# Attention and MoE in one kernel: from which tile on scores and value products use split operands

## The chip, the cores and the metric

One core of a Trainium2 chip runs the whole kernel. The time is that of the device for one execution, in microseconds; the median of several executions counts.

## The reference

Eight batches of eight heads go through attention with a window and a few global positions, and the result through a small MoE-like layer:

```python
s_g = scale * q_g @ concat(k_g, k_l).T          # 32 global queries see all 544 keys
out_g = softmax(s_g) @ concat(v_g, v_l)
s_ll = where(abs(i - j) <= 32, scale * q_l @ k_l.T, -1e9)   # 512 local queries, window 32
s_l = concat(scale * q_l @ k_g.T, s_ll)          # and the 32 global keys
out_l = softmax(s_l) @ concat(v_g, v_l)
x = concat(out_g, out_l).transpose(0, 2, 1, 3).reshape(8 * 544, 512)
h = maximum(maximum(x @ w1, x @ w2), x @ w3)     # w1, w2, w3: 512 x 768
out = h @ w_out                                  # 768 x 512
```

All operands are float32.

## The kernel before, in words

The attention runs over 128 tiles (`sl` from 0 to 127). A tile is 128 queries of a pair of heads (`p = sl // 4`, the place in it `t = sl % 4`); four pairs make a batch. For a tile there are four steps on PE, each ahead of the next by one or more tiles: `scores(sl + 3)`, `trans(sl + 1)` (transposes the softmax, which went to the buffer `prob` by DMA), `transg(sl + 1)` (the same for the softmax of the global queries, from `probg`) and `pv(sl)` (the product with the values). `glob(p + 1)` makes the global scores of the next pair in two parts, `glob_soft` its softmax: the smallest value `nmg`, the exponential, its sum `zg` with a reciprocal, a scaling, and six DMAs to `probg`.

Between these steps `fill(n)` puts matmuls of the MoE layer of the batch before, 18 a tile, from tile 16 on. The weights of that layer come in as float32 and are split into a high and a low part on the way (`convert`): ACT at L165, four DVE steps at L168 to L171, ACT at L178, POOL at L182. These conversions go on, one or two a tile, up to tile 25, and the last ones are those of w_out.

A float32 product can be made in two ways here. Native: operands stay float32, and PE takes each matmul in two records (lines L273, L315, L383). Split: an operand is first divided into a high part, rounded to the faster format, and a low part, the difference; PE then multiplies these (L277, L319, L390). `split_q`, `split_k` and `split_v` divide the queries, keys and values: a cast on ACT (`copy`) and a subtraction on POOL or DVE (`sub`, L94). With a split value product the transposed softmax is divided too (`trans` and `transg`: a second step on DVE, from PSUM), and the result's parts are added: a copy `lox` on ACT, one add at L396 and two at L398 on DVE in place of one copy of the result.

Two numbers say where the change from native to split takes place: `NATK`, the tiles with native scores (the global scores of a pair go with its first tile), and `NAT`, the first tile with a split value product.

`copy`, `sub` and `times` choose the engine with the least load by a table of costs. The order of instructions on each engine is set when the program is built, by priorities and the layer's own estimates of what is ready, so it is not that of the code, and it moves when the work changes. Each engine works strictly through its row; the DMAs are all issued from SP's queue, in its order.

Of the kernel before, what the change touches and what calls it, by code (L numbers as in the profile page):

```python
# [22 lines left out]
KW = 576  # L23
NEG = -8.0e9

NATK = range(0, 28)
HIMAX = float(np.array(0x47EFFFFF, np.int32).view(np.float32))


# [22 lines left out]
def body(ctx, tc, kin, qin, vin, min_, w1, w2, w3, w4, out):  # L52
# [43 lines left out]
    def copy(out, a, psum=False):  # L96
        n = width(out)
        c = {"d": n * (1.04 if psum else 0.52) + (160 if psum else 150), "a": n * 0.833 + (150 if psum else 190)}
        if least(c) == "d":
            dve.tensor_copy(out=out, in_=a)  # L100
        else:
            act.copy(out=out, in_=a)  # L102
# [103 lines left out]


    NS = 4 * B * NP
    NAT = 26
    EARLY, AHEAD = 16, 9  # L210
    kraw, kst, qraw, qs, vraw, vs, xr, sc, pg, pts = [{} for _ in range(10)]

    def load_k(p):
        if p < B * NP:
            if 4 * p in NATK:
                kraw[p] = att.tile([128, KW + 2 * SG], F32, name="kn", tag="kst")
# [4 lines left out]
    def split_k(p):  # L221
        if p >= B * NP or 4 * p in NATK:
            return
        r = kraw.pop(p)
        g = r[:, KW:].rearrange("p (j g) -> p j g", j=2)
        t = qgz
        copy(t[:, :, 0:SG], g)
        sub(t[:, :, 64:64 + SG], g, f32(t)[:, :, 0:SG])
        t = kst[p] = att.tile([128, 2, KW], F32R, name="kst")
        copy(t[0:64, 0], r[0:64, 0:KW])  # L230
        copy(t[64:128, 1], r[64:128, 0:KW])
        sub(t[64:128, 0], r[0:64, 0:KW], f32(t)[0:64, 0])
        sub(t[0:64, 1], r[64:128, 0:KW], f32(t)[64:128, 1])

    def load_q(s):
        if s < NS:
            if s in NATK:
                qraw[s] = att.tile([128, 256], F32, name="qn", tag="qs", bufs=4)
# [4 lines left out]
    def split_q(s):  # L243
        if s < NS and s not in NATK:
            r = qraw.pop(s)
            t = qs[s] = att.tile([128, 2, 256], F32R, name="qs", bufs=4)
            copy(t[:, 0], r)
            sub(t[:, 1], r, f32(t)[:, 0])
# [6 lines left out]
    def split_v(s):  # L255
        if NAT <= s < NS:
            v = vraw.pop(s)
            t = vs[s] = att.tile([128, 4, 2, D], F32R, name="vs")
            copy(t[:, :, 0], v)
            sub(t[:, :, 1], v, f32(t)[:, :, 0])  # L260

    def glob(p, step):
# [7 lines left out]
        ps = psS.tile([128, 512], F32, name="S")  # L270
        if 4 * p in NATK:

# [27 lines left out]
    def scores(sl):  # L300
# [11 lines left out]
        for j in range(2):  # L312
            if sl in NATK:

# [19 lines left out]
    def trans(sl):  # L334
# [11 lines left out]
        src = ps.rearrange("p (x q) -> p x q", q=128)  # L346
        if sl < NAT:
            pt = pts[sl] = att.tile([128, 2, 2, 160], F32, name="pt", tag="pt")
# [7 lines left out]
    def transg(sl):  # L356
# [7 lines left out]
        src = g[:, 64 * h:64 * h + 64 * n].rearrange("p (c j g) -> p c j g", j=2, g=SG)  # L364
        if sl < NAT:
            copy(pt.rearrange("p j c q -> p c j q")[:, 0:n, :, 128:160], src, True)
# [6 lines left out]
    def pv(sl):  # L373
# [3 lines left out]
        if t == 0:  # L377
            xr[p] = xp.tile([128, 4, 160], F32, name="xr")
        if sl < NAT:

# [211 lines left out]
```

## Time and profile before

| | |
|---|---|
| median of 3 runs | 859.42 us (859.35 to 860.28) |
| profiled execution | 863.26 us, its span 861.4 us |
| mean granted clock of PE | 0.973 |
| PE busy | 813.0 us, 94% of the span |
| DVE, ACT, POOL busy | 566.7, 529.1, 509.8 us |

The profile is of one execution. Busy time of PE counts matmuls that overlap, so a busy PE is not PE at its peak. "PEld" is PE's loading of the stationary operand. The chain of waits follows the work that ended last back in time, at each step to what released it. A row of a timeline gives start and length in microseconds, the engine, the line, the operation, and in brackets how long the engine was idle before it and what ended that.

### The profile page before, as it was taken

Reading aid. Unit: us, or ns where it says so; the run is one execution under the profiler, and the core shown is the slowest. Engines: PE = TensorE matmul, PEld = TensorE weight load, DVE = VectorE, ACT = ScalarE, POOL = GpSimd, SP = SyncE. Lnnn points to the kernel's source line nnn. Section 1 sums busy time; section 2 is a strip of 40 time slices with the busy share of each in tenths; the row PEclk is TensorE's granted clock in tenths of the full one; section 3 lists DMA queues with packets and bytes.
Section 4 is the critical chain, followed back from the end, with each engine's and each line's share of the span. In section 5 each row is a group of like instructions: output and inputs, shape, how many; then the busy total and the mean of one; then the engine's idle time right before and its main releaser. Section 6 shows DMA issues by size and latency. Waiting matters only on the chain.

```text
span 861.4 us, 15721 instructions
## 1 busy us (share of the span) xinstructions
PE 813.0 (94%) x4452; PEld 674.2 (78%) x4452; DVE 566.7 (66%) x1784; ACT 529.1 (61%) x1479; POOL 509.8 (59%) x683
## 2 busy tenths in 40 slices
PE   5866788999999999999999999999999999999997
PEld 3644566778888788888888888888888888888896
DVE  4657699787777677777778677867787676511111
ACT  4656566677767676767776767776776766511111
POOL 4535577786667666776768576766677664411211
PEclk8786999999999999999999999999999999999999
DMA  6586655424333533344333533353334322100000
GB/s 201 166 243 186 190 165 190 146 90 153 103 106 96 160 112 106 100 123 125 104 109 100 150 98 100 96 160 111 112 111 131 121 75 72 62 24 1 25 25 25
DMA packets 107238, 98.53 MB, mean 114 GB/s; under 512 B 21008, under 2 KB 97936, under 8 KB 107152
## 3 DMA queue, kind: packets, MB, share of 16 engines
q1 hardware_dynamic: 107152, 97.53, 37.2%
q8 instruction: 36, 0.59, 0.3%
q14 instruction: 50, 0.41, 0.2%
HBM read 56.85 MB, written 8.91 MB: 76 GB/s over the span
## 4 chain that ended last, share of the span: by engine, by line
PE 82%; DVE 6%; DMA 6%; ACT 2%; issue 2%; SPq 2%; POOL 1%; ACTq 0%; POOLq 0%; DVEq 0%
PE pm L421 45%; PE pm L440 16%; PE O L390 6%; PE S L319 5%; PE T L342 4%; DMA wraw<-w_in 2%; PE S L277 1%; DVE wraw L170 1%; DMA probg<-sg 1%; PE O L383 1%; PE S L363 1%; PE pm L315 1%; DMA early<-s 1%; ACT s L324 1%; PE S L315 1%
## 5 line engine op out<-in xcount | busy, mean ns | idle before, releaser
L421 PE MATMUL pm<-xs,wh 128*128 128x512 f32 (+1 forms) x1296 | 408.0, 388 | 3.3 <-POOL xs L94 3.3
L421 PEld LDWEIGHTS pm<-xs,wh 128*128 128x128 f32 x1296 | 233.6, 189 | 35.3 <-POOL xs L94 3.8
L421 PE MATMUL pm<-xs,wl 128*128 128x512 f32 (+1 forms) x648 | 253.1, 391 | 0.0
L112 POOL TENSOR_SCALAR s<-s,z 128x192 f32<-128x192 f32 (+1 forms) x250 | 113.0, 465 | 98.7 <-ACT lox L102 37.8
L421 PEld LDWEIGHTS pm<-xs,wl 128*128 128x128 f32 x648 | 122.5, 189 | 22.7 <-issue 1.6
L324 ACT ACTIVATE s<-s,nm 128x192 f32<-128x192 f32 (+1 forms) x256 | 118.0, 462 | 26.6 <-DVE nm L322 22.6
L440 PE MATMUL pm<-woh,h 128*128 128x512 f32 x408 | 133.7, 398 | 0.1
L94 POOL TENSOR_TENSOR h<-m,h 128x512 fp32r<-128x512 f32 (+1 forms) x54 | 69.3, 1283 | 95.4 <-ACT h L102 93.9
L429 DVE TENSOR_TENSOR m<-pm,m 128x512 f32<-128x512 f32 (+1 forms) x108 | 71.1, 659 | 72.2 <-PE pm L421 72.0
L94 POOL TENSOR_TENSOR qs<-qraw,qs 128x256 fp32r<-128x256 f32 x100 | 73.8, 749 | 56.3 <-ACT qs L102 45.3
L94 DVE TENSOR_TENSOR pt<-T,pt 128x512 fp32r<-128x512 f32 x102 | 70.5, 691 | 46.4 <-ACT pt L102 44.5
L322 DVE CUSTOM_DVE_ANT_0 s<-S,mask 128x192 f32<-128x192 f32 (+1 forms) x232 | 77.9, 371 | 18.5 <-PE S L315 7.7
L326 DVE TENSOR_SCALAR z<-z 128x2 f32<-128x2 f32 x128 | 52.0, 406 | 49.8 <-ACT s L324 49.2
L440 PEld LDWEIGHTS pm<-woh,h 128*128 128x128 f32 x408 | 74.7, 188 | 12.1 <-POOL h L94 0.5
L440 PE MATMUL pm<-wol,h 128*128 128x512 f32 x204 | 81.8, 401 | 0.0
L94 POOL TENSOR_TENSOR vs<-vraw,vs 128x256 fp32r<-128x256 f32 x102 | 75.8, 744 | 8.2 <-ACT vs L102 4.0
L94 POOL TENSOR_TENSOR kst<-kraw,kst 64x576 fp32r<-64x576 f32 x49 | 70.4, 1436 | 11.8 <-issue 8.2
L102 ACT CAST pt<-T 128x512 fp32r<-128x512 f32 x90 | 52.7, 586 | 36.0 <-PE T L342 36.0
L102 ACT CAST qs<-qraw 128x256 fp32r<-128x256 f32 x100 | 40.5, 407 | 54.8 <-PE S L319 54.3
L390 PEld LDWEIGHTS O<-pt,vs 128*128 128x128 f32 x408 | 66.4, 188 | 9.1
L390 PE MATMUL O<-pt,vs 128*128 128x320 f32 (+1 forms) x408 | 72.8, 300 | 0.0
L342 PEld LDWEIGHTS T<-identr,prob 128*128 128x128 f32 x448 | 50.5, 141 | 25.1 <-DMA prob<-s 2.6
(95 smaller groups left out, 1292.2 us busy)
## 6 DMA issues: line engine op xcount, KB each, us to landing
vraw<-v_in SPq DMA_DIRECT2D x128, 128.0 KB, 2.4
qraw<-q_in SPq DMA_DIRECT2D x100, 128.0 KB, 2.2
prob<-s SPq DMA_DIRECT2D x56, 224.0 KB, 2.4
prob<-s SPq DMA_DIRECT2D x56, 192.0 KB, 2.3
wraw<-w_in SPq DMA_DIRECT2D x18, 512.0 KB, 5.3
out_dram<-o SPq DMA_DIRECT2D x32, 256.0 KB, 2.6
kraw<-k_in SPq DMA_DIRECT2D x25, 320.0 KB, 3.1
qn<-q_in SPq DMA_DIRECT2D x28, 128.0 KB, 3.4
```

The costliest lines, as they stand in the source:

```text
L94: (dve if least(c) == "d" else pool).tensor_tensor(out=out, in0=a, in1=b, op=ALU.subtract)
L102: act.copy(out=out, in_=a)
L112: pool.tensor_scalar(out=out, in0=a, scalar1=col, scalar2=1.0, op0=ALU.mult, op1=ALU.mult)
L319: pe.matmul(ph[j][:, 0:n], lhsT=qs[sl][:, a, 128 * j:128 * j + 128], rhs=kst[p][:, j, c0:c0 + n], start=(a == 0), stop=(a == 1))
L322: dve.tensor_tensor_reduce(out=s[:, j, 0:n], in0=ph[j][:, 0:n], in1=mask[:, (1, 0, 1, 0)[t], 32 * (t == 0):32 * (t == 0) + n], scale=-0.12 ...
L324: act.activation(out=s[:, j, 0:n], in_=s[:, j, 0:n], func=AF.Exp, bias=nm[:, j:j + 1], scale=-1.0, accum_out=z[:, j:j + 1])
L326: dve.tensor_scalar(out=z, in0=z, scalar1=1e-9, scalar2=None, op0=ALU.add)
L342: i = pe.transpose(pr[:, 256 * j + 128 * c:256 * j + 128 * c + 128], s[:, j, 128 * c:128 * c + 128], identr)
L390: pe.matmul(o[:, j, 0:320].rearrange("p (a q) -> p a q", a=2)[:, :, 0:n], lhsT=vs[sl][:, 2 * j + c].rearrange("p a d -> p (a d)"), rhs=pt[ ...
L421: pe.matmul(ps[:, 0:n], lhsT=w[f][:, i, k], rhs=xs[k][:, a, 0:n], start=(q == 0), stop=(q == 11))
L429: dve.tensor_tensor(out=m[:, 0:n], in0=ps[:, 0:n], in1=m[:, 0:n], op=ALU.max)
L440: pe.matmul(ps, lhsT=hh[f][:, a, 128 * t:128 * t + 128], rhs=w[:, f], start=(q == 0), stop=(q == 17))
```

## The change

Value products are split from tile 22 on in place of tile 26, scores from tile 24 on in place of tile 28. So the value products of tiles 22 to 25, the scores of tiles 24 to 27 and the global scores of pair 6 change from native to split; the host prepares the inputs to match.

```diff
-NATK = range(0, 28)
+NATK = range(0, 24)
...
-    NAT = 26
+    NAT = 22
```

The order of the instructions moves around these tiles. Three places follow; the numbers at the names are those of buffers.

DVE, before, from the scores of tile 25 (`s_1485`) on; `zg_1356` belongs to the global softmax of pair 6, `z_1487` to the softmax of tile 25, `wct` and `wraw` to a weight conversion:

```order
L171 SCALAR_TENSOR_TENSOR wct_1456<-wraw_1310 128x512
L322 ISA s_1485,nm_1486<-S_1484,mask_89 128x224
L322 ISA nm_1486 128x1
L291 TENSOR_SCALAR zg_1356<-zg_1356 64x1
L292 RECIPROCAL zg_1356<-zg_1356 64x1
L326 TENSOR_SCALAR z_1487<-z_1487 128x2
L327 RECIPROCAL z_1487<-z_1487 128x2
```

DVE, after, from behind the same L322 of tile 25 on; `zg_1366` is now that of pair 6, `lox_1552` and `xr_1358` are parts of the value product of tile 22, `pt_1502` is the transposed softmax of tile 23:

```order
L396 TENSOR_TENSOR lox_1552<-O_1547,lox_1552 64x320
L289 TENSOR_TENSOR nmg_1365<-nmg_1365 64x1
L94 TENSOR_TENSOR pt_1502<-S_1571,pt_1502 128x2x2x32
L326 TENSOR_SCALAR z_1515<-z_1515 128x2
L398 TENSOR_TENSOR xr_1358<-O_1547,lox_1552 64x160
L327 RECIPROCAL z_1515<-z_1515 128x2
L398 TENSOR_TENSOR xr_1358<-O_1547,lox_1552 64x160
L168 TENSOR_SCALAR wct_1493<-wct_1493 128x512
L169 TENSOR_SCALAR wct_1493<-wct_1493 128x512
L291 TENSOR_SCALAR zg_1366<-zg_1366 64x1
L170 SCALAR_TENSOR_TENSOR wraw_1400<-wraw_1400,wct_1493 128x512
L292 RECIPROCAL zg_1366<-zg_1366 64x1
```

L291 stood right behind L322 of tile 25 before; nine rows are between them now, and one more between L291 and L292. The step `nmg` (L289) came a dozen rows ahead of that L322 and now follows it.

PE, before, behind the value product of tile 23; L363 is the transpose from `probg` for tile 24, L342 that of tile 25 from `prob`, the L421 rows are MoE matmuls:

```order
L421 MATMUL pm_1595<-xs_872,wl3_111 128x512
L421 MATMUL pm_1595<-xs_932,wh3_105 128x512 x2
L363 MATMUL S_1608<-identr_87,probg0_94 128x128
L421 MATMUL pm_1595<-xs_932,wl3_111 128x512
L421 MATMUL pm_1595<-xs_989,wh3_105 128x512 x2
L421 MATMUL pm_1595<-xs_989,wl3_111 128x512
L342 MATMUL T_1629<-identr_87,prob1_93 128x128 x4
L421 MATMUL pm_1638<-xs_813,wh4_106 128x512 x2
L421 MATMUL pm_1638<-xs_813,wl4_112 128x512
L421 MATMUL pm_1638<-xs_872,wh4_106 128x512
L315 MATMUL S_1643<-kn_899,qn_1341 128x192 x2
```

PE, after, from the same place of the MoE layer on; L319 are the scores of tile 27, as L315 was:

```order
L421 MATMUL pm_1642<-xs_872,wl3_111 128x512
L421 MATMUL pm_1642<-xs_932,wh3_105 128x512 x2
L421 MATMUL pm_1642<-xs_932,wl3_111 128x512
L421 MATMUL pm_1642<-xs_989,wh3_105 128x512 x2
L421 MATMUL pm_1642<-xs_989,wl3_111 128x512
L342 MATMUL T_1684<-identr_87,prob1_93 128x128 x4
L421 MATMUL pm_1694<-xs_813,wh4_106 128x512 x2
L421 MATMUL pm_1694<-xs_813,wl4_112 128x512
L421 MATMUL pm_1694<-xs_872,wh4_106 128x512 x2
L363 MATMUL S_1659<-identr_87,probg0_94 128x128
L319 MATMUL S_1699<-kst_1178,qs_1634 128x192 x4
```

L363 of tile 24 moved behind nine MoE matmuls and the transpose of tile 25, to just ahead of the scores of tile 27.

SP's queue, before, at the transfers to `probg0` for pair 6 (L298) and the softmax of tile 25 (L330):

```order
L298 DMA probg0_94<-sg_1354 64x128
L330 DMA prob1_93<-s_1485 128x2x224
L298 DMA probg0_94<-sg_1354 64x96 x2
L298 DMA probg0_94<-sg_1354 64x64
L298 DMA probg0_94<-sg_1354 64x96
```

SP's queue, after, at the same transfers; L160 loads a piece of w_out:

```order
L330 DMA prob1_93<-s_1513 128x2x224
L160 DMA wraw_1485<-wo_in 128x512
L298 DMA probg0_94<-sg_1364 64x128
L298 DMA probg0_94<-sg_1364 64x96 x2
L298 DMA probg0_94<-sg_1364 64x64
```

The softmax of tile 25 and a weight load are now ahead of the six transfers to `probg0`.

## The prediction

> **What bounds the kernel now.** I read the page's slices first, then the busy time by stage, then the chain of waits where the stages differ, then each engine's timeline at the tiles that the change touches. On the page, PE (TensorE's matmuls) runs at 5 to 8 tenths in the first eight slices and at 9 afterwards; DVE (VectorE) peaks in slices 6 and 7.
>
> ```profile
> PE   5866788999999999999999999999999999999997
> DVE  4657699787777677777778677867787676511111
> ```
>
> Busy time in four stretches (length, then PE, PEld, DVE, ACT, POOL busy with their instructions, granted PE clock, DMA share, GB/s):
>
> ```profile
> 105.00:130.00 25.00, 21.00 (x112) 15.06 (x110) 21.63 (x48) 16.63 (x42) 18.05 (x17) 1.00 0.59 183
> 130.00:150.00 20.00, 17.99 (x100) 13.56 (x100) 18.04 (x36) 12.59 (x31) 14.10 (x15) 1.00 0.57 183
> 150.00:165.00 15.00, 12.60 (x67) 9.85 (x67) 11.12 (x31) 9.98 (x27) 9.38 (x11) 0.89 0.45 139
> 182.00:205.00 23.00, 22.92 (x127) 18.90 (x127) 16.98 (x58) 16.22 (x46) 17.18 (x23) 1.00 0.44 135
> ```
>
> From 182 us on PE is full, so every microsecond by which PE reaches that stage later or earlier is one at the end. The tiles of the change (22 to 27) are worked on from about 130 to 165 us, where DVE, converting weights beside attention, is the fullest engine. The chain of waits (start, length, what) there runs through DVE and ends on PE at one place:
>
> ```profile
> 143.19 1.15 DVE wraw L170
> 144.65 1.37 DVE wct L171
> 147.50 0.89 POOL s L112 x2
> 150.49 1.82 DMA probg<-sg
> 152.40 0.25 PE S L363
> ```
>
> The PE timeline shows that place: L363, the transpose of the global softmax of pair 6 for tile 24, waits 2.71 us for its DMA. It is the longest stall between 105 and 165 us. The scores of tile 27 (L315) follow at 156.05.
>
> ```profile
> 130.77 0.53 PE L342 MATMUL T<-identr,prob 128*128 128x128 f32 x4 [2.12 <-DMA prob<-s]
> 152.40 0.25 PE L363 MATMUL S<-identr,probg 128*128 128x128 f32 x1 [2.71 <-DMA probg<-sg]
> 156.05 1.07 PE L315 MATMUL S<-kn,qn 128*128 128x192 f32 x4
> ```
>
> **The change, part by part: PE.** A native score tile takes 0.59 us of PE issue (113.80 to 114.39), a split one 0.42 (162.79 to 163.21). A native value product takes 0.64 (157.99 to 158.63) and I take 0.12 as the gain of the split one, a little below the scores' 0.17.
>
> ```profile
> 113.80 0.92 PE L315 MATMUL S<-kn,qn 128*128 128x224 f32 x4
> 114.39 0.56 PE L421 MATMUL pm<-xs,wh 128*128 128x512 f32 x1
> 162.79 0.59 PE L319 MATMUL S<-kst,qs 128*128 128x192 f32 x4
> 163.21 0.41 PE L421 MATMUL pm<-xs,wh 128*128 128x512 f32 x1
> 157.99 0.71 PE L383 MATMUL O<-pt,vraw 128*64 128x160 f32 x8
> 158.63 0.62 PE L277 MATMUL S<-kst,qgz 128*128 128x384 f32 x2
> ```
>
> Four tiles of each save 4 x 0.17 + 4 x 0.12 = 1.2 us, and the global scores of pair 6 a few tenths. What lies ahead of L363 (scores 24 to 26, products 22 and 23, the global scores) is worth nothing, because PE waits there anyway; that wait is its cover. Only scores 27 and products 24 and 25 count: 0.17 + 0.24 = 0.4 us less.
>
> **What the other engines get.** Groups of instructions (busy us, mean ns, then idle before):
>
> ```profile
> L94 DVE TENSOR_TENSOR pt<-T,pt 128x512 fp32r<-128x512 f32 x102 | 70.5, 691 | 46.4 <-ACT pt L102 44.5
> L94 DVE TENSOR_TENSOR pt<-S,pt 128x128 fp32r<-128x128 f32 x51 | 14.5, 284 | 0.7
> L94 DVE TENSOR_TENSOR pt<-S,pt 128x64 fp32r<-128x64 f32 x51 | 11.5, 225 | 2.1
> L396 DVE TENSOR_TENSOR lox<-O,lox 64x320 f32<-64x320 f32 x102 | 48.3, 474 | 10.7 <-ACT lox L102 7.5
> L398 DVE TENSOR_TENSOR xr<-O,lox 64x160 f32<-64x160 f32 x204 | 64.3, 315 | 3.4
> L94 POOL TENSOR_TENSOR vs<-vraw,vs 128x256 fp32r<-128x256 f32 x102 | 75.8, 744 | 8.2 <-ACT vs L102 4.0 <-DVE vs L100 2.6 <-DVE z L326 1.6
> L94 POOL TENSOR_TENSOR qs<-qraw,qs 128x256 fp32r<-128x256 f32 x100 | 73.8, 749 | 56.3 <-ACT qs L102 45.3 <-DVE nm L322 7.5 <-DMA probg<-sg 2.2
> L94 POOL TENSOR_TENSOR kst<-kraw,kst 64x576 fp32r<-64x576 f32 x49 | 70.4, 1436 | 11.8 <-issue 8.2
> ```
>
> Each split value product adds to DVE 0.69 (low part of the weights from T), 0.23 or 0.28 (from S), 0.47 (lox) and 2 x 0.315 (xr): 2.05 us, over four tiles 8.2. POOL gets 4 x 0.744 for values, 4 x 0.749 for queries and 2 x 1.436 for the keys of pair 6: 8.8 us. ACT gets the matching casts and loses xr copies; it is busy 12.59 of 20 us at 130 to 150, and I cost it at nothing.
>
> What these do to the end is decided at L363. Its DMA needs the reciprocal of the global sum (zg, L291 and L292), which stands in DVE's row behind the scores of tile 25 (L322). DVE and its neighbours there:
>
> ```profile
> 129.20:146.30 17.10, 14.60 (x83) 11.45 (x83) 16.93 (x32) 10.30 (x27) 12.30 (x12) 1.00 0.60 193
> 138.29 0.41 DVE L168 TENSOR_SCALAR wct<-wct 128x512 f32<-128x512 f32 x1
> 139.93 0.68 DVE L170 SCALAR_TENSOR_TENSOR wraw<-wraw,wct 128x512 int32<-128x512 int32 x1
> 140.54 1.51 DVE L169 TENSOR_SCALAR wct<-wct 128x512 int32<-128x512 int32 x1
> 145.94 0.38 DVE L322 CUSTOM_DVE_ANT_0 s<-S,mask 128x224 f32<-128x224 f32 x1
> 146.25 0.14 DVE L291 TENSOR_SCALAR zg<-zg 64x1 f32<-64x1 f32 x1
> 140.04 1.72 POOL L94 TENSOR_TENSOR h<-m,h 128x512 fp32r<-128x512 f32 x1 [0.64 <-ACT h L102]
> 149.06 3.30 SPq L298 DMA_DIRECT2D probg<-sg  x5
> 153.09 0.38 SPq L160 DMA_DIRECT2D wraw<-wo_in  x1
> ```
>
> One earlier link of the chain, and the usual time of such a transfer on the page:
>
> ```profile
> 98.60 7.17 DMA wraw<-w_in
> wraw<-w_in SPq DMA_DIRECT2D x18, 512.0 KB, 5.3
> ```
>
> DVE is busy 16.93 of 17.10 us from 129.2 to 146.3: what is put in comes out later. The steps to the landing of that DMA, by the new order:
>
> 1. Ahead of L322 of tile 25 DVE now has the low parts of tiles 22 and 23 from T and of tile 22 from S: 2 x 0.69 + 0.23 = 1.6. The small nmg step leaves (0.14, as L291): +1.5.
> 2. POOL's additions near DVE. The row at 140.54 shows a DVE step of 0.41 us (as L168 at 138.29) stretched to 1.51 while POOL's 140.04 row runs. Added close by are two value splits and one query split net (2.2 us), and earlier the keys of pair 6 and two query splits (4.4 us). Ends: +6.6 if each microsecond of POOL delays DVE by one; below nothing, down to -1.9, since on SP's queue the key load of pair 6 moves from just ahead of the 98.60 weight load, which took 7.17 us where 5.3 is usual, to a place before the transfers ahead of it. Loads keep their number and size. I take +1.0, nearer to nothing, since POOL is busy only 18.05 of 25 us before 130 and 14.10 of 20 after.
> 3. Between L322 of tile 25 and zg now stand lox 0.47, three small steps (3 x 0.15), the S part of tile 23 0.28, xr 2 x 0.315, L168 and L169 (2 x 0.41): 2.7. One L170 (0.68) comes between zg and its reciprocal: +3.3.
> 4. On SP's queue a weight load (0.38) is now ahead of the six probg transfers: +0.4.
>
> The transfers land 6.2 us later, and L363 runs at 152.4 + 6.2 = 158.6 in place of 152.4. But PE's order moved too: the eight MoE matmuls and the transpose of tile 25 that came between L363 and the scores of tile 27 (3.65 us, 152.40 to 156.05) now stand ahead of L363, and one matmul more (0.2). The scores of tile 27 start at 158.7, 2.6 later, and the matmul makes it 2.4.
>
> 5. The clock. After the 2.71 us wait the granted clock is low (length, PE busy, clock, DMA, GB/s):
>
> ```profile
> 152.30:156.90 4.60, 4.50 (x18) 0.63 0.48 156
> ```
>
> That loses 4.6 x 0.37 = 1.7 us. After the 2.12 us wait at 130.77 it was not low (1.00 for 130 to 150). PE now meets two waits there, for tile 25's softmax and at L363, where it met one. A second loss is 0 to 1.7; I take 0.9, the middle, as the two waits shown differ.
>
> Sum: 2.4 + 0.9 - 0.4 = +2.9, told as +3. After that DVE gets 4.1 us for tiles 24 and 25 where it is busy 11.12 of 15; this leaves 3.9, so 0 to +1, of which I count 0. The profiled execution took 863.26 us (span 861.4 and 1.9 around it), 3.84 above the median of the runs, 859.42. The sum gives 866.3 for such an execution and 862.4 for the median.
>
> The Trainium skill ("SBUF — State Buffer", section "SBUF: two separate sides") says that DVE and GpSimd share one port pair as an exclusive lock, held for a whole instruction, and that the loser fully blocks. The 140.54 row agrees. By that rule alone step 2 would be its upper end, +6.6 in place of +1.0, and the time 868.
>
> **The rivals.** Changes within 0.2% (1.7 us) can hardly be told from none.
>
> *Faster.* DVE's row contains waiting for POOL (1.1 us in the 140.54 row alone). The added DVE steps read PSUM, and if they run while POOL is at work they take the place of that waiting; the conversions come out earlier. Then steps 1 and 2 sum to about -1.9 instead of +2.5, the transfers land 1.8 us later instead of 6.2, PE has its moved work as cover, the wait stays under 2.12 us and the clock is not lowered. The scores of tile 27 start at 154.3, 1.8 earlier; with 0.2 for the matmul, 0.4 for PE's savings and 0.3 for the low clock beyond 156.05 that is -2.7, 856.7. It decides from a landing about 3.3 us later than now. Against it: 16.93 of 17.10 busy, and step 3 stays.
>
> *No change that can be told.* Steps 1 and 2 cancel, the landing is 3.7 us later, and PE's moved work pays for it: with the clock and PE's savings +0.5, 859.9.
>
> *Clearly slower.* Each POOL addition delays DVE by most of its length: step 2 is +5, the landing 10.2 us later, the scores of tile 27 6.4 later; with the clock and the saving +6.9, 866.3. This is a mechanism of its own, POOL's work in DVE's way. For it: the stretched row. Against it: POOL's idle time before 130 us.
>
> *Nothing happens,* because the splits hide and PE is full only later: that is the second case.
>
> **How the numbers follow.** Forecast (+1.7 to +5) 0.38, clearly slower 0.14, no change 0.25, faster 0.23. The likeliest gives 862.4. The range starts at 856.4, just below the faster rival, and ends at 867.4, one past the clearly slower case; about one in ten is left out on either side. The forecast alone reaches from 861.1 to 864.4. So faster 0.23, same 0.25, slower 0.52.
>
> **What would show it.** In the changed profile L363 of tile 24 should wait for probg at about 158 us, the transpose of tile 25 just before it for prob, zg should start about 5 us later than 146.25, and PE should be full from about 168 us on. L363 without a wait would make the forecast wrong on the fast side; stretched L168 to L171 rows (mean above 1 us) or two low-clock stretches, on the slow side.

## The result, and the profile after

The changed kernel takes 868.01 us (median of 4 runs, 867.28 to 869.60), the kernel before 859.38 in the runs beside it: ratio 1.0102, 95% interval 1.0086 to 1.0118, 8.6 us slower. The forecast was 862.4 with a range up to 867.4. The profiled execution took 868.56, its span 866.4, mean granted clock 0.969.

The page's slices of the changed kernel, PE and DVE:

```profile
PE   5866877799999999999999999999999999999997
DVE  5577689886778677777787677867777677511111
```

PE now has 7 tenths in slices 6 to 8 (108 to 173 us) and DVE 8, 9 and 8 in slices 6 to 8: the weak stage has become longer. The stretches shown of before, now (length, then PE, PEld, DVE, ACT, POOL busy, granted clock, DMA share, GB/s):

```profile
105.00:130.00 25.00, 20.07 (x105) 15.22 (x105) 22.16 (x45) 15.45 (x40) 16.48 (x17) 0.93 0.58 192
130.00:150.00 20.00, 15.11 (x74) 11.21 (x73) 18.47 (x40) 13.15 (x36) 17.37 (x18) 0.93 0.46 149
150.00:165.00 15.00, 11.23 (x44) 8.73 (x44) 12.75 (x29) 8.45 (x22) 9.11 (x9) 0.76 0.38 116
182.00:205.00 23.00, 22.66 (x125) 18.69 (x124) 16.90 (x57) 16.43 (x48) 18.16 (x24) 1.00 0.43 128
```

PE loses 2.9 us of work at 130 to 150 (17.99 before), and the granted clock is lowered in three stretches where it was in one. PE's timeline of the changed kernel, the rows with the long waits (in brackets) and the scores of tile 27 at 158.16:

```profile
111.23 1.02 PE L315 MATMUL S<-kn,qn 128*128 128x224 f32 x4 [1.58 <-DVE nm L322]
119.28 0.51 PE L342 MATMUL T<-identr,prob 128*128 128x128 f32 x4 [2.91 <-DMA prob<-s]
135.13 0.28 PE L363 MATMUL S<-identr,probg 128*128 128x128 f32 x1 [2.33 <-DVE nm L322]
147.05 1.20 PE L319 MATMUL S<-kst,qs 128*128 128x224 f32 x4 [1.06 <-DVE nm L322]
158.02 0.34 PE L363 MATMUL S<-identr,probg 128*128 128x128 f32 x1 [3.08 <-DMA probg<-sg]
158.16 1.13 PE L319 MATMUL S<-kst,qs 128*128 128x192 f32 x4
172.15 0.28 PE L363 MATMUL S<-identr,probg 128*128 128x128 f32 x1 [1.88 <-DVE nm L322]
```

The forecast knew one of them, at 158.02. Two come before any tile whose scores or product are split (111 and 119 us, the scores of tile 22 and the softmax of tile 21), but behind the split of pair 6's keys, whose subtractions run on POOL at 95.34 and 98.61. Four name DVE's L322: the next user of a PSUM buffer `S` (scores, transposed global softmax, global scores; there are two such buffers) waits until DVE has read the scores that are in it.

**What the first profile hid.** There is a second profile of the kernel before:

> The kernel before, unchanged, for a second profile. If the first profile lost about 3.3 us in the loading stage by chance, this one shows the value product of tile 15 at about 81 us in place of 84.36 and a span near 857.5; the order of instructions and the waits from 105 to 165 us are then the undisturbed ones to compare with. If the loss belongs to the kernel before, it is there again.

It took 857.18 us, span 855.3. One row each for the stage from the value product of tile 15 to that of tile 28: the first profile of the kernel before, the second, and the changed kernel.

```profile
84.36:182.30 97.94, 84.60 (x451) 63.65 (x450) 77.81 (x192) 61.86 (x164) 67.85 (x71) 0.97 0.55 171
```

```profile
81.19:177.80 96.61, 84.41 (x450) 63.78 (x450) 78.61 (x193) 62.71 (x165) 68.11 (x73) 0.96 0.54 172
```

```profile
81.12:187.93 106.81, 86.98 (x435) 66.78 (x435) 89.59 (x210) 68.15 (x179) 74.62 (x81) 0.92 0.49 156
```

The first profile had reached tile 15 3.2 us late, in the loading stage, where the programs hardly differ. The two first spans (861.4 and 866.4) therefore show 5.0 us, the medians 8.6. In the stage itself the changed kernel is 8.9 to 10.2 us longer, and that is the whole difference: behind it the three spans have 679.1, 677.5 and 678.5 us left.

**The stage as a sum.** Below, "waits" is the sum of the brackets of PE's rows in this stage, "low clock" the sum over 50 equal windows of length times one minus the granted clock, "rest" what is left. A wait that lies in a low-clock stretch counts in both (0.65 us in the changed kernel, none in the two of before, up to 1.7 in e5). One profiled execution each; the ratio is that of all timed runs to those of the kernel before beside them.

| kernel | ratio (95%) | stage | waits | low clock | rest |
|---|---|---|---|---|---|
| before, first and second profile | | 97.9, 96.6 | 13.3, 12.2 | 3.4, 3.4 | 81.2, 81.0 |
| changed | 1.0102 (1.0086 to 1.0118) | 106.8 | 19.8 | 8.5 | 78.5 |
| e1 products alone | 1.0050 (1.0035 to 1.0066) | 101.4 | 15.8 | 5.1 | 80.6 |
| e2 scores alone | 1.0093 (1.0067 to 1.0119) | 105.4 | 18.3 | 8.6 | 78.6 |
| e3 changed, low parts by ACT, not POOL | 1.0154 (1.0125 to 1.0183) | 108.2 | 20.8 | 10.8 | 76.6 |
| e4 changed, pt low parts by ACT, not DVE | 1.0093 (1.0060 to 1.0126) | 106.2 | 20.0 | 8.5 | 77.8 |
| e5 changed, subtractions by DVE, not POOL | 1.0110 (1.0085 to 1.0134) | 107.3 | 20.7 | 10.3 | 76.4 |
| e6 before, L182 by DVE | 1.0015 (0.9999 to 1.0032) | 99.9 | 12.6 | 5.1 | 82.2 |
| e8 before, extra POOL work | 1.0027 (1.0011 to 1.0043) | 99.5 | 13.7 | 5.1 | 80.7 |
| e9 before, extra ACT and POOL work | 1.0025 (1.0012 to 1.0038) | 100.5 | 13.9 | 5.1 | 81.5 |
| e10 changed, later conversions | 1.0072 (1.0047 to 1.0097) | 105.2 | 17.7 | 10.2 | 77.3 |
| e12 before, later conversions | 1.0028 (1.0009 to 1.0046) | 100.7 | 13.6 | 5.1 | 82.0 |
| e11 splits later | 0.9988 (0.9971 to 1.0005) | 96.4 | 11.3 | 1.7 | 83.5 |
| e15 before, conversions behind scores | 1.0076 (1.0046 to 1.0106) | 100.3 | 12.2 | 7.8 | 80.2 |
| e16 changed, the same | 1.0102 (1.0052 to 1.0153) | 102.5 | 17.8 | 6.8 | 77.9 |
| e17 before, other fill | 0.9997 (0.9978 to 1.0016) | 96.2 | 10.9 | 4.8 | 80.5 |
| e18 changed, the same | 1.0082 (1.0050 to 1.0114) | 104.7 | 19.2 | 6.8 | 78.7 |
| e19 scores alone, one load later | 1.0113 (1.0091 to 1.0135) | 107.0 | 20.8 | 6.8 | 79.4 |
| e20 changed, one load later | 1.0160 (1.0137 to 1.0183) | 108.7 | 21.9 | 8.5 | 78.2 |

Against the second profile the changed kernel has 7.6 us more of waits, 5.1 more of low clock and 2.5 less of the rest, of which 0.65 is the time counted twice.

### The profile page after: what moved, and what is told of

It reads as the page before. It is cut to its first block, busy times and chain, and to the rows that moved or that the text cites. A ratio compares the mean times of both kernels' runs of the same rounds, so it can differ in the third digit from the quotient of the medians.

```text
span 866.4 us, 15756 instructions
## 1 busy us (share of the span) xinstructions
PE 814.1 (94%) x4436; PEld 677.2 (78%) x4436; DVE 578.9 (67%) x1801; ACT 534.2 (62%) x1496; POOL 516.9 (60%) x693
## 4 chain that ended last, share of the span: by engine, by line
PE 79%; DVE 4%; DMA 3%; ACT 2%; POOL 2%; issue 2%; SPq 0%; ACTq 0%; POOLq 0%; DVEq 0%
PE pm L421 45%; PE pm L440 16%; PE O L390 6%; PE S L319 5%; PE T L342 3%; PE S L277 1%; DVE wraw L170 1%; PE S L363 1%; DMA prob<-s 1%; PE S L315 1%; POOL s L112 1%; DMA wraw<-w_in 1%; DVE wct L171 1%; POOL xs L94 0%; DMA wraw<-wo_in 0%
## 5 line engine op out<-in xcount | busy, mean ns | idle before, releaser
L421 PE MATMUL pm<-xs,wh 128*128 128x512 f32 (+1 forms) x1296 | 408.1, 388 | 3.2 <-POOL xs L94 3.2
L421 PEld LDWEIGHTS pm<-xs,wh 128*128 128x128 f32 x1296 | 234.3, 190 | 35.8 <-POOL xs L94 3.6
L421 PE MATMUL pm<-xs,wl 128*128 128x512 f32 (+1 forms) x648 | 253.4, 391 | 0.0
L112 POOL TENSOR_SCALAR s<-s,z 128x192 f32<-128x192 f32 (+1 forms) x250 | 110.8, 456 | 91.2 <-ACT lox L102 38.0
L421 PEld LDWEIGHTS pm<-xs,wl 128*128 128x128 f32 x648 | 123.1, 190 | 21.6 <-issue 0.6
L324 ACT ACTIVATE s<-s,nm 128x192 f32<-128x192 f32 (+1 forms) x256 | 117.9, 461 | 25.7 <-DVE nm L322 20.8
L94 POOL TENSOR_TENSOR qs<-qraw,qs 128x256 fp32r<-128x256 f32 x104 | 77.3, 754 | 55.2 <-ACT qs L102 41.6
L94 DVE TENSOR_TENSOR pt<-T,pt 128x512 fp32r<-128x512 f32 x106 | 73.2, 690 | 48.3 <-ACT pt L102 45.8
L322 DVE CUSTOM_DVE_ANT_0 s<-S,mask 128x192 f32<-128x192 f32 (+1 forms) x232 | 77.7, 370 | 11.8 <-PE S L315 5.4
L440 PEld LDWEIGHTS pm<-woh,h 128*128 128x128 f32 x408 | 74.6, 188 | 12.3 <-POOL h L94 0.8
L94 POOL TENSOR_TENSOR vs<-vraw,vs 128x256 fp32r<-128x256 f32 x106 | 78.6, 742 | 9.0 <-ACT vs L102 5.3
L94 POOL TENSOR_TENSOR kst<-kraw,kst 64x576 fp32r<-64x576 f32 x52 | 74.7, 1437 | 15.0 <-issue 7.2
L102 ACT CAST pt<-T 128x512 fp32r<-128x512 f32 x95 | 55.4, 583 | 37.2 <-PE T L342 37.2
L390 PEld LDWEIGHTS O<-pt,vs 128*128 128x128 f32 x424 | 69.8, 190 | 10.9 <-POOL h L94 1.3
L390 PE MATMUL O<-pt,vs 128*128 128x320 f32 (+1 forms) x424 | 76.6, 302 | 0.6 <-DVE pt L94 0.6
L102 ACT CAST qs<-qraw 128x256 fp32r<-128x256 f32 x104 | 42.3, 408 | 53.1 <-PE S L319 48.4
L319 PEld LDWEIGHTS S<-kst,qs 128*128 128x128 f32 x416 | 62.5, 192 | 11.6 <-DVE nmg L281 1.6
```

The source lines that it names most:

```text
L94: (dve if least(c) == "d" else pool).tensor_tensor(out=out, in0=a, in1=b, op=ALU.subtract)
L112: pool.tensor_scalar(out=out, in0=a, scalar1=col, scalar2=1.0, op0=ALU.mult, op1=ALU.mult)
L319: pe.matmul(ph[j][:, 0:n], lhsT=qs[sl][:, a, 128 * j:128 * j + 128], rhs=kst[p][:, j, c0:c0 + n], start=(a == 0), stop=(a == 1))
L322: dve.tensor_tensor_reduce(out=s[:, j, 0:n], in0=ph[j][:, 0:n], in1=mask[:, (1, 0, 1, 0)[t], 32 * (t == 0):32 * (t == 0) + n], scale=-0.12 ...
L324: act.activation(out=s[:, j, 0:n], in_=s[:, j, 0:n], func=AF.Exp, bias=nm[:, j:j + 1], scale=-1.0, accum_out=z[:, j:j + 1])
L390: pe.matmul(o[:, j, 0:320].rearrange("p (a q) -> p a q", a=2)[:, :, 0:n], lhsT=vs[sl][:, 2 * j + c].rearrange("p a d -> p (a d)"), rhs=pt[ ...
```

## The experiments

Theories at first: V, DVE's own added work costs; P, POOL's added work holds up DVE; O, the late global softmax at L363. Later: W, the added work fills the stage, wherever it is put; C, it is what waits for the splits and the order that comes with them, and of that C2, the order of the rows, against D, the split work itself in any order.

**Half of the change each.** e1 is the kernel before with `NAT = 22`, e2 the kernel before with `NATK = range(0, 24)`.

> The kernel before with one of the two edits alone: value products are split from tile 22 on, scores stay native up to tile 27. Theory V (DVE's added 8.2 us for four split value products, in a stage where DVE is full, carry the cost): +6 to +8 us against the kernel before, nearly the whole 8.6. Theory P (POOL's added subtractions block DVE's steps; of their 8.8 us only the 3.0 for values are left here): +2 to +3.5. Theory O (the cost is made by the late global softmax of pair 6 and the order around L363 alone): +3 to +4 if L363 of tile 24 still waits more than 2.7 us for probg, and about 0 if it doesn't. All three expect scores of tile 24 to 27 to add two or three tenths less here than in the changed kernel.

> The kernel before with the other edit alone: scores are split from tile 24 on, value products stay native up to tile 25. Theory V: 0 to +1.5 us, as DVE gets nothing. Theory P: +4 to +6, since 5.8 of POOL's 8.8 added us (keys of pair 6, queries of tiles 24 to 27) stay, ahead of and in the conversions. Theory O: 0 to +1, as DVE's row at the global softmax gets no new steps. If the two halves sum to much less or more than 8.6 us, they act on each other.

e1 cost 4.3 us (1.0050 of 858.4), e2 8.0. Theory V falls: the half that gives DVE nothing costs nearly all. Theory P had e2 at 4 to 6. The halves sum to 12.3, more than 8.6, so they act on each other; both stop PE at L363 of tile 22 (2.55 us in e1, 2.28 in e2, 2.33 in the changed kernel). In e1 L363 of tile 24 waited 1.25 us only, where theory O asked for a cost of about 0: it falls too.

**The added work moved to another engine.** In e3, e4 and e5 a helper takes the place of `sub` for the tiles of the change: a plain `act.copy` of the high part's source in e3 (keys, queries, values) and e4 (pt), a `dve.tensor_tensor` subtraction in e5 (keys, queries, values). e3 and e4 thus leave those low parts out of the result:

```diff
-            sub(t[:, 1], r, f32(t)[:, 0])
+            low(t[:, 1], r, f32(t)[:, 0], s < 28)
...
-        sub(lo, src, f32(hi), True)
+        low(lo, src, f32(hi), sl < 26, True)
```

> The changed kernel, but the low parts that the change newly asks of POOL (queries of tiles 24 to 27, keys and global queries of pair 6, values of tiles 22 to 25) are written by a plain copy on ACT in place of a subtraction on POOL; the low parts' values are left out of the computation thereby. POOL is back at its load of before, ACT gets some 7 us more, DVE keeps its additions. Theory P: most of the cost goes, +1 to +2 us against the kernel before is left. Theory V: +6 to +8 stay. If ACT becomes the bound (it is busy 15.5 of 25 us at 105 to 130), the L102 casts run late and the run is as slow or slower; the trace will show that as waits on ACT.

> The changed kernel, but the low parts of the transposed softmax of tiles 22 to 25 (pt from T and from S) are written by a plain copy on ACT in place of a subtraction on DVE; those low parts' values are left out of the computation thereby. DVE loses 4 x (0.69 + 0.25) = 3.8 of its 8.2 added us, POOL keeps its additions. Theory V: the cost falls by about half, to +4 or less. Theory P: +7 to +8 stay, since what blocks DVE is unchanged.

> The changed kernel, with nothing left out, but the subtractions that the change newly asks of POOL (queries of tiles 24 to 27, keys and global queries of pair 6, values of tiles 22 to 25) are made by DVE. By the table of costs in the kernel each takes DVE 0.38 us for 256 elements and 0.71 for 576, 4.5 us in all, in place of 8.8 us on POOL. Theory V (DVE's own work in its full stage is what costs, one for one): +11 to +13 us against the kernel before, worse than the changed kernel. Theory P (POOL's subtractions hold up DVE's steps, so that one of 0.74 us costs DVE more than doing it itself): below the changed kernel, +4 to +6.

e3 cost 13.2 us in place of the 1 to 2 that P asked for, e4 8.0 in place of V's 4 or less, e5 9.4, between the two and not told from the changed kernel. To take the added work off POOL brings nothing, and to put 3.8 us less on DVE brings nothing. Both theories that hang on one engine's load fall. That the load only moved on to ACT is not quite excluded for e3 and e4; in e3's stage PE's waits name ACT for 0.7 us in all.

**POOL's and ACT's part alone.** e8 adds to the kernel before POOL subtractions that nothing reads; e9 puts an ACT cast ahead of each, as a split has it. e6 takes L182 from POOL.

```diff
+        if 24 <= s < 28:
+            act.copy(out=waste, in_=qraw[s])        # e9 only
+            pool.tensor_tensor(out=waste, in0=qraw[s], in1=waste, op=ALU.subtract)
...
-        pool.tensor_tensor(out=dl, in0=f32(c), in1=f32(dh), op=ALU.subtract)   # e6: L182
+        dve.tensor_tensor(out=dl, in0=f32(c), in1=f32(dh), op=ALU.subtract)
```

> The kernel before, with native scores and products where it has them, and with extra subtractions on POOL whose result nothing reads: four of 64x256 where the keys of pair 6 are handled and one of 128x256 for each of the queries of tiles 24 to 27, about 6 us of POOL in all, as the split scores ask of it (the run with split scores alone cost +8). Theory P: +4 to +8 us against the kernel before. Theory V, and any theory in which the split scores' casts, copies and order are what costs: 0 to +1.5.

> The kernel before, native scores and products as there, with the extra work of the split scores on ACT and POOL: where the queries of tiles 24 to 27 and the keys of pair 6 are handled, a cast on ACT and a subtraction on POOL whose result nothing reads (eight of each, about 3 us of ACT and 6 of POOL). POOL's part alone cost +2.2. Theory W (the added work fills the stage in which DVE and ACT have little slack): +5 to +8 us, as the split scores did. Theory C (it is that the scores now wait for casts and subtractions, and the row orders that come with it): +2 to +3.5, little more than POOL's part.

> The kernel before, but the subtraction that ends each weight conversion (L182, 1.29 us and more on POOL, 29 or so of them) is made by DVE (0.64 us by the table of costs). Theory V: DVE is full and gets 0.64 us for each of some 12 conversions between 105 and 165 us, so +5 to +8 us against the kernel before. Theory P: each of them holds up DVE by up to 1.29 us now, so 0 to -6 us.

e8 cost 2.3 us, e9 2.1, e6 1.3 (its interval reaches none). So the extra casts and subtractions of keys and queries, with nothing waiting for them, account for about 2 of e2's 8 us; in e8 and e9 PE's matmuls all stand in the order of before. e6 is far from V's 5 to 8 and shows none of the gain that P allowed. Theory W falls, C stands. One of e9's casts on ACT and the subtraction behind it on POOL:

```profile
97.66 0.39 ACT L229 CAST waste<-kn 64x256 bf16<-64x256 f32 x1
98.13 0.67 POOL L231 TENSOR_TENSOR waste<-kn,waste 64x256 bf16<-64x256 f32 x1 [0.84 <-ACT waste L229]
```

**Conversions later, and the splits later.** e10 (changed) and e12 (before) stretch the list of conversion steps to tile 27; e11 goes the other way, `NAT = 30` and `NATK = range(0, 32)`.

```diff
-    WS = [..., 1, 2, 2, 1, 2, 2, 1, 2, 2, 1, 2, 2]
+    WS = [..., 1, 2, 2, 1, 2, 1, 2, 1, 2, 1, 2, 1, 1, 1]
```

> The changed kernel, with the last steps of the weight conversion a little later: from tile 19 on one or two a tile down to tile 27 in place of two of three tiles with two down to tile 25 (four fewer steps by tile 25 at the most). Theory W: the stage of tiles 18 to 25 is relieved of some 5 us of DVE, so two or three of PE's stalls over 1.5 us and their low clock windows (1.7 us each) go: +3 to +6 us against the kernel before in place of +8.6. Theory C: +7 to +9 as before. If the w_out conversions come too late for their use at tile 28, PE stalls near 180 us and it is slower than +9.

> The kernel before with the same later conversions as in the run of the changed kernel with later conversions. Theory W: the waits at the softmax of tile 22 (2.1 us) and for probg (2.7 us) shrink, one or both low clock windows go: -1 to -4 us. Theory C: 0. This is the candidate for a version better than both.

> The change in the other direction: value products split from tile 30 on, scores from tile 32 on, against 26 and 28 in the kernel before. PE pays about 1.5 us more for native tiles where it is full (4 x 0.17 + 4 x 0.12 and the global scores). DVE, POOL and ACT lose 8, 9 and some 5 us from 165 to 200 us and nothing before 150. Theory W and theory C: 0 to +2 us, as the stage that stalls is not relieved. If a trend holds by which each tile costs 2 us the earlier it is split: -4 to -8.

e10 cost 6.2 us against the kernel before, e12 2.4, where a gain was hoped for, and e11 gained 1.0 with an interval that reaches none: no version here is shown to beat the kernel before. Theory W had 3 to 6 for e10 and a gain for e12, theory C 7 to 9 and 0: e12 fits neither. The trend by which a tile split earlier costs 2 us each falls with e11. The same edit took some off the one kernel and added some to the other; their distance is 4.5 us (865.15 and 860.63) in place of 8.6.

**The same work in another order.** e15 (before) and e16 (changed) write the conversion steps of a tile behind the next tile's scores; e17 and e18 deal out one MoE matmul a tile behind the value product (`fill(4)` and `fill(3)` around it changed places).

```diff
+        for _ in range(WS[sl - 1] if 0 < sl <= len(WS) else 0):
+            weight_step()
         if t == 2:
             split_k(p + 2)
...
-        for _ in range(WS[sl] if sl < len(WS) else 0):
-            weight_step()
```

> The kernel before with the same work in another order: the weight conversion steps of a tile are written behind the next tile's scores (a few lines later in the loop), so that DVE's L322 comes ahead of conversion steps that stood before it. Theory C2 (the order of the rows on DVE and PE decides how often PE waits): differs from the kernel before by 2 us or more, -2 to -4 if the scores' L322 come earlier as meant. Theory D (the split scores' own casts, subtractions and reads cost it, whatever the order): 0 to -1.

> The changed kernel with the same edit. Theory C2: the waits of L315 and L363 for DVE's L322 (at 111, 135, 147 and 172 us in the changed kernel) go or shrink, with one to three low clock windows of 1.7 us: +1 to +5 us against the kernel before. Theory D: +7 to +9, its distance to the kernel before with this edit stays 8 to 9.

> The kernel before with one of 18 MoE matmuls of each tile dealt out behind the value product in place of ahead of it; no work is added or taken. Theory C2: a change of some size either way, -3 to +4 us, with the number of low clock windows. Theory D: within 1 us of the kernel before.

> The changed kernel with the same edit. Theory C2: anywhere between +3 and +10 us against the kernel before, and not the same distance as between the unedited kernels. Theory D: +8 to +9.

e15 cost 6.5 us, where a gain was meant, with the work of the kernel before (a few copies and subtractions change engine): order alone can cost three quarters of what the change does. Against the second profile of before 3.4 us were lost ahead of tile 15 and 3.6 in the stage. e16 took 4.4 us off the changed kernel's stage (102.5 for 106.8) and lost it again ahead of tile 15 (85.19 for 81.12); as a whole it cost 8.8 us, where C2 had 1 to 5. The kernel before and the changed one are 3.4 us apart in this order (865.02 and 868.45), 7.8 in that of e17 and e18 (858.63 and 866.38). The 3.4 is rough: e16's four runs lie between 863.62 and 870.29, and one of them is below all of e15's. So theory D, by which the distance stays at 8 to 9, is not borne out in one pair and about holds in the other.

**One load.** On SP's queue the load of pair 6's keys is what first stands elsewhere in the changed kernel: its raw buffer is free, where the native keys waited for the buffer of pair 4. e19 (scores alone) and e20 (changed) issue it a tile later:

```diff
-            load_k(p + 3)
+        if t == (3 if p == 3 else 2):
+            load_k(p + 3)
```

> Split scores alone (as the run that cost +8), but the load of pair 6's keys is issued a tile later, at tile 15 in place of 14. On SP's queue it then stands two rows behind its place in the kernel before, not seven ahead of it; the row order of PE differs from the kernel before first at the 109th row in place of the 97th, that of DVE at the 269th in place of the 205th. The work is that of the split scores. Theory C2 (the order carries the cost): the stalls at the scores of tile 22 and the softmax of tile 20 (1.67 and 2.57 us) with a low clock window behind them go, value products 17 to 20 take about 22.5 us as before in place of 25.6: +2 to +5 us in all. Theory D (the split work itself): +7 to +9.

> The changed kernel with the same one load a tile later. Theory C2: the stalls at 111 and 119 us go with a low clock window, +3 to +6 us against the kernel before in place of +8.6; what is left is then the added work of both parts. Theory D: +8 to +9.

They cost 9.7 and 13.7 us: a miss for theory C2 in the form that the early order carries the cost, and e20, at 11.8 or more by its interval, one for theory D (8 to 9) as well. The early part came as expected: value products 17 to 20 took 23.6 us in e19 (98.29 to 121.84), 22.3 in the second profile of before, 25.6 in e2, and the waits at 112 and 120 us (1.67 and 2.57 in e2, the second that of tile 21's softmax) shrank to 0.47 and 1.63. But the next weak place took back more. PE in e19, then DVE and POOL there:

```profile
136.47 0.30 PE L363 MATMUL S<-identr,probg 128*128 128x128 f32 x1 [4.24 <-DVE nm L322]
...
126.38 1.42 DVE L326 TENSOR_SCALAR z<-z 128x2 f32<-128x2 f32 x1 [1.60 <-ACT s L324]
129.79 1.79 DVE L170 SCALAR_TENSOR_TENSOR wraw<-wraw,cut 128x512 int32<-128x512 int32 x1
133.56 1.71 DVE L170 SCALAR_TENSOR_TENSOR wraw<-wraw,wct 128x512 int32<-128x512 int32 x1
135.19 0.34 DVE L322 CUSTOM_DVE_ANT_0 s<-S,mask 128x192 f32<-128x192 f32 x1
136.06 0.34 DVE L322 CUSTOM_DVE_ANT_0 s<-S,mask 128x192 f32<-128x192 f32 x1
...
126.33 1.44 POOL L94 TENSOR_TENSOR kst<-kraw,kst 64x576 fp32r<-64x576 f32 x1
129.56 1.47 POOL L94 TENSOR_TENSOR kst<-kraw,kst 64x576 fp32r<-64x576 f32 x1
133.45 1.26 POOL L182 TENSOR_TENSOR wl<-cut,wh 128x512 fp32r<-128x512 f32 x1 [1.27 <-ACT wh L178]
```

The scores of tile 24 started at 128.78, but seven conversion steps stood ahead of their L322, three DVE rows were stretched beside a POOL row, and both `S` buffers stayed taken until 136.4. The same place in the second profile of the kernel before, with its native scores started at 128.44:

```profile
127.43 1.63 DVE L168 TENSOR_SCALAR wct<-wct 128x512 f32<-128x512 f32 x1
129.96 0.36 DVE L322 CUSTOM_DVE_ANT_0 s<-S,mask 128x192 f32<-128x192 f32 x1
130.85 0.35 DVE L322 CUSTOM_DVE_ANT_0 s<-S,mask 128x192 f32<-128x192 f32 x1
```

There L322 came 1.5 us behind the scores, here 6.4. This wait of L363 of tile 22 for L322, at 131 to 138 us, took 1.97 to 5.18 us in the 11 profiles with the early products or scores. In five of the 9 others it is not there, in four it is shorter (0.28 in e12, 0.49 in e17, 0.74 in e15, 1.40 in e9), so its size tells the two groups apart.

## Why the prediction was wrong

The sign was right and the size not: +3 forecast, +8.6 measured. By its own steps:

- **The place.** L363 of tile 24 was forecast at 158.6 and ran at 158.02, the scores of tile 27 at 158.7 and 158.16. That is luck in part: the execution had reached tile 15 3.2 us earlier than the one from which the sum started. Counted from there the scores of tile 27 are 5.4 us later (77.04 for 71.69), not 2.6.
- **The step that failed: where the sum began and ended.** It began at the low parts ahead of tile 25's L322. By the value product of tile 20 the changed kernel was already 3.1 us behind (42.88 us from tile 15, 39.82 before), with the two new waits at 111 and 119 us on the way. The splits of pair 6's keys, which come first, stood in the sum as part of step 2's +1.0 only, as a delay at L363. From tile 20 to the scores of tile 27 it lost 2.3 more, near the forecast's 2.6, and behind them another 3.5. So 6.6 of the 8.9 us of the stage lie outside the stretch that the sum priced. The value product of tile 20 before, then PE, DVE and POOL of the changed kernel: a conversion step beside the keys' subtraction, and one that stands between the two halves of L322 of tile 21, for which the scores of tile 22 waited at 111.23:

```profile
124.18 0.71 PE L383 MATMUL O<-pt,vraw 128*64 128x160 f32 x8
```

```profile
124.00 0.71 PE L383 MATMUL O<-pt,vraw 128*64 128x160 f32 x8
...
98.73 1.58 DVE L168 TENSOR_SCALAR cut<-cut 128x512 f32<-128x512 f32 x1
108.83 0.38 DVE L322 CUSTOM_DVE_ANT_0 s<-S,mask 128x224 f32<-128x224 f32 x1
109.14 1.73 DVE L171 SCALAR_TENSOR_TENSOR cut<-wraw 128x512 int32<-128x512 int32 x1
110.79 0.38 DVE L322 CUSTOM_DVE_ANT_0 s<-S,mask 128x224 f32<-128x224 f32 x1
...
98.61 1.42 POOL L94 TENSOR_TENSOR kst<-kraw,kst 64x576 fp32r<-64x576 f32 x1
109.05 1.28 POOL L182 TENSOR_TENSOR wl<-cut,wh 128x512 fp32r<-128x512 f32 x1 [2.22 <-ACT wh L178]
```

- **Steps 1 and 3 (DVE's row).** Right in kind. zg came 6.9 us later, counted from tile 15 (61.89 and 68.77), where 5 was forecast, and its reciprocal 1.85 behind it, where 0.68 was counted, since a POOL row ran beside L170. DVE and POOL of the changed kernel:

```profile
149.89 0.13 DVE L291 TENSOR_SCALAR zg<-zg 64x1 f32<-64x1 f32 x1
150.00 1.81 DVE L170 SCALAR_TENSOR_TENSOR wraw<-wraw,wct 128x512 int32<-128x512 int32 x1
151.74 0.15 DVE L292 RECIPROCAL zg<-zg 64x1 f32<-64x1 f32 x1
...
149.98 1.29 POOL L182 TENSOR_TENSOR wol<-wct,woh 128x512 fp32r<-128x512 f32 x1 [0.29 <-ACT woh L178]
```

- **Step 2 (POOL beside DVE, +1.0).** As a price it was low by about 1: e8 and e9 measured 2.1 to 2.3 for some 6 us of POOL. The rule by which every microsecond of POOL costs DVE one gave 868, the measured time, but for another reason. DVE's conversion steps and small steps (those of z, zg and nmg) ran 17.0 us over their undisturbed lengths (0.69 us for L170 and L171, 0.42 for L168 and L169, 0.16 for the small ones) in the stage of the second profile, where POOL was busy 68.1 us. It was 16.8 in e9 with POOL busy 74.9, 22.1 in the changed kernel with 74.6, 21.9 in e5 with 69.4 and 23.8 in e3 with 64.6. The Trainium skill ("SBUF — State Buffer", section "SBUF: two separate sides") is right that a DVE step can be held up by a POOL row, as the L170 above (1.81 us beside 1.29 of POOL) shows; the sum over a stage doesn't follow POOL's load.
- **Step 4** held: the transfers followed a weight load at 152.57.
- **Waits that nobody had: PSUM.** The waits of L315, L363, L319 and L363 for L322 (1.58, 2.33, 1.06, 1.88) are no step of the sum. DVE's later row was followed only to zg, not to the next user of the `S` buffers.
- **Step 5, the clock, +0.9.** Of the terms of the sum it was mis-sized most: 5.1 measured, from 3.4 to 8.5 us. The forecast allowed one more low stretch in the place it looked at; there were three more in the stage.
- **DVE for tiles 24 and 25, counted 0:** the wait at 172.15 (1.88) and a low stretch at 158 to 164 twice as long fall there. These are the 3.5 us from the scores of tile 27 to the value product of tile 28 (8.9 less 5.4).
- **PE's savings, 0.4:** 2.5 of rest in the stage, 1.8 without what is counted twice; where waits are counted apart, all of the cheaper matmuls count. By the rows at full clock these make some 1.5: 0.11 a product (0.64 and 0.53), 0.09 or 0.15 a score tile, 0.57 for the global scores of a pair (1.11 and 0.54), which the forecast put at a few tenths. Its 0.17 for a score tile set a native one of 128x224 beside a split one of 128x192; for the scores of tile 27 it is 0.09 (0.51 and 0.42).
- **Rivals.** "Clearly slower" (866.3) was nearest in time; its mechanism, each POOL addition in DVE's way, is worth about 2, so that is luck. The signs named for the slow side came: two and more low-clock stretches, L170 and L171 at means of 1.02 and 1.00 us from tile 15 to 27. The transpose of tile 25 did not wait, and PE was full from 174 us on, not 168.

What stays open is why the time is lost: under one and the same edit the changed kernel is 3.4 to 8.6 us behind the kernel before, and the extra casts and subtractions of keys and queries, in PE's old order, cost 2.1 to 2.3. What lies between changes with the order of the rows, and that the order makes it, not the waiting for split operands, is argued, not shown. Which row decides could not be shown; the one that looked like it, the load of the keys, did not.

## What to carry to other kernels

Where a stage has no slack on an in-order engine, follow its delay to every buffer that it frees, not just to the wait that is longest now, and start the sum at the first row that is new or stands elsewhere, not at the tile where the new operands are used. Let the range hold a low clock stretch for each new stall: here, against the second profile, six stalls of 1.06 to 2.91 us were new and two of 1.44 and 1.98 gone, and the stage had three stretches more. Before a change is charged with a cost, time both versions in a second order of the same work: here the distance was 3.4 to 8.6 us.

## What the runs showed of the hardware

Here the low clock comes in pieces of one size. In 17 of the 20 stages the loss is within 0.07 us of a multiple of 1.71 us (3.41 = 2, 5.12 = 3, 6.83 = 4, 8.53 = 5, 10.24 = 6 pieces). The changed kernel in windows of 2 us, around the 1.06 us wait that ends at 147.05 and the 3.08 us one that ends at 158.02:

```profile
146.00:148.00 2.00, 0.95 (x4) 0.95 (x5) 2.00 (x6) 1.48 (x5) 1.96 (x3) 0.77 0.14 48
148.00:150.00 2.00, 2.00 (x7) 1.61 (x6) 1.90 (x8) 2.00 (x6) 1.06 (x3) 0.50 0.48 135
150.00:152.00 2.00, 2.00 (x10) 1.79 (x10) 2.00 (x4) 0.40 (x2) 1.26 (x1) 0.88 0.33 115
...
158.00:160.00 2.00, 1.98 (x7) 1.81 (x8) 2.00 (x4) 1.40 (x3) 0.85 (x1) 0.50 0.40 129
160.00:162.00 2.00, 1.38 (x5) 0.78 (x4) 2.00 (x3) 0.00 (x1) 1.92 (x2) 0.50 0.48 137
162.00:164.00 2.00, 2.00 (x8) 1.80 (x7) 1.34 (x5) 1.18 (x4) 0.66 (x2) 0.50 0.15 23
```

The first is half clock for about 3.4 us (2 x 0.23 + 1.0 + 2 x 0.12 = 1.70 lost), the second, two such pieces on end (3.42 lost from 156 to 166). The Trainium skill ("TensorE: Matmul & The Clock Gate", "Part 1: The HAM clock gate") gives a window of 3.413 us and a half rate, which agrees. It says that the rate falls after an idle window of that length; here it fell behind shorter waits too, such as the 1.06 us above with one of 1.09 us 2.6 us ahead of it, and not behind each: the second profile of the kernel before kept 1.00 from 146 to 154, past this one:

```profile
148.64 0.25 PE L363 MATMUL S<-identr,probg 128*128 128x128 f32 x1 [2.39 <-DMA probg<-sg]
```
